# Splitting every load of q, k and v from one DMA of four heads (256 KB) into two of two heads (128 KB)

## Chip, cores, metric

One core of a Trainium2 chip. The metric is the device time of one execution in microseconds (us), as the median of several runs; the profile of one execution is read beside it. On one core a run is called slow when it lies more than 1.5% above the fastest run of the same kernel. Ratios use fast runs alone.

## The reference, cut to what matters

Linear attention with decay over 4 batches, 8 heads, 768 positions and 64 columns, in blocks of 64 with a running state per head, then a highway layer with two 512 x 512 weights. Everything is float32 in and out.

```python
for b in range(nb):
    qb, kb, vb = (q[:, :, sl], k[:, :, sl], v[:, :, sl])
    intra = einsum('bhij,bhjd->bhid', einsum('bhic,bhjc->bhij', qb, kb) * Dmask, vb)
    inter = einsum('bhid,bhde->bhie', qb * lam_pow, kv_state)
    out[:, :, sl] = intra + inter
    kv_state = lam_block * kv_state + einsum('bhsd,bhse->bhde', kb * rev_pow, vb)
...
H = np.maximum(x @ w_h, 0.0); T = 1.0 / (1.0 + np.exp(-(x @ w_t + b_t)))
return T * H + (1.0 - T) * x
```

## The kernel before

The work is cut into 12 stages of 256 positions and all 8 heads. Each stage loads 512 KB each of q, k and v, in two DMAs of 256 KB. Another engine casts a tile to bf16 (kb, qb, vs), and TensorE then transposes and multiplies. The first two stages are handled in halves of four heads; later stages have one tile of eight heads each, with five buffers. All loads and stores go through SyncE's DMA queue, in a fixed order written by hand: all loads first, with the eight weight loads among them, and then the 25 stores.

```python
def load(x, src, n, p, hs):
    b, c = divmod(n, NST)
    for h in range(hs.start, hs.stop, 4):
        nc.sync.dma_start(out=get(x, n, p)[:, h - hs.start:h - hs.start + 4, :],
                          in_=src[b, h:h + 4, c * 2 * C:(c + 1) * 2 * C, :].rearrange("h (p j) d -> p h (j d)", j=J))
...
def fill(eng):      # TensorE's warm-up, 12 times, before the first data arrive
    for i in range(2):
        T.matmul(get("fill")[:, i], lhsT=id128, rhs=id128[:, None, :].to_broadcast([128, NP, 128]), start=True, stop=True)
...
LA = 5              # buffers of a load tile
```

The layer that builds the program gives the DMAs of SyncE and ScalarE eight semaphores in turn; an issue waits until the DMA eight places before it has landed. So eight are in flight at most.

## Time and profile before

| | before |
|---|---|
| time | 113.19 us median (113.16 to 113.62) |
| span in the profile | 110.9 us |
| DMAs issued by SyncE until the last load | 80 |
| last load's issue ends | 72.5 us |
| median from issue to landing of a load | 5.4 us |

How to read it: SyncE's track shows how long it takes to hand a DMA to the queue, not how long the data move. The table of slices shows how full the DMA engines are. The two together tell whether the issue or the engines set the pace. The lines are in the prediction. Some words used there: a DMA lands when its data have arrived and its semaphore, a counter that other engines wait on, says so; a descriptor is one contiguous run of bytes in a DMA, 512 bytes in a load of q, k or v; push-back means that an issue is drawn out because the DMA engines have not yet taken the earlier work; the slack of a tile is the time between its being ready and its first use.

### The profile page before, as it was taken

The page shows a single profiled execution, that of the slowest core. Times are in us where ns is not written, and L with a number is a line of the kernel's source. Part 1 is how long each engine was busy: PE and PEld are TensorE (multiplying, and loading weights), DVE is VectorE, ACT ScalarE, POOL GpSimd, SP SyncE. Part 2 cuts the span into 40 slices and gives each one's busy share as a digit, 9 for nine tenths or more (in the row PEclk, how much of TensorE's full clock was granted, in tenths as well). Part 3 has the DMA queues.
Part 4 walks back from the last instruction along what each step waited for, and adds up shares of the span by engine and source line. Part 5 has one row for each costly group of instructions (what it writes and reads, how often), then busy time and mean ns, then how long its engine had stood idle before and what let it go on. Part 6 is the DMA issues. An engine that isn't in the chain of part 4 may idle for free.

```text
span 110.9 us, 4776 instructions
## 1 busy us (share of the span) xinstructions
PE 101.5 (92%) x2073; PEld 86.3 (78%) x2073; DVE 78.4 (71%) x128; ACT 72.9 (66%) x137; POOL 63.5 (57%) x55
## 2 busy tenths in 40 slices
PE   4996489689999999999999999999999999999960
PEld 1353469578889889888888889999899888889950
DVE  0179896684998899797778854788775797764630
ACT  3574443177288967668695788787878844785780
POOL 6004626263469899988979979899940040401420
PEclk9999965559999999999999999999999999999998
DMA  0999999999999999999999999999995250024263
GB/s 10 267 292 290 290 293 287 293 356 320 253 290 297 288 292 292 290 294 289 293 287 287 279 292 295 292 264 370 392 343 204 107 188 0 6 101 183 101 236 142
DMA packets 43964, 27.57 MB, mean 249 GB/s; under 512 B 1828, under 2 KB 41000, under 8 KB 43944
## 3 DMA queue, kind: packets, MB, share of 16 engines
q1 hardware_dynamic: 43792, 27.27, 88.3%
q8 instruction: 16, 0.26, 1.0%
q14 instruction: 4, 0.03, 0.1%
q10 hardware_dynamic: 152, 0.01, 0.1%
HBM read 20.98 MB, written 6.29 MB: 246 GB/s over the span
## 4 chain that ended last, share of the span: by engine, by line
PE 76%; SPq 11%; DMA 6%; DVE 2%; issue 1%; POOLq 1%; ACT 0%; DVEq 0%
PE w L293 39%; SPq L208 11%; PE w L315 10%; PE w L223 10%; DMA kf<-in_k_dram 6%; PE w L239 5%; PE o L264 5%; PE kv L272 4%; PE o L252 4%; DVE qT L175 1%; POOLq L469 1%; DVE kb L175 1%; DVE hmx L297 0%; ACT o_sb L173 0%; DVEq L175 0%
## 5 line engine op out<-in xcount | busy, mean ns | idle before, releaser
L293 PE MATMUL w<-xT,w_b 128*128 128x256 bf16 (+1 forms) x416 | 46.9, 265 | 0.0
L293 PEld LDWEIGHTS <-w_b 128*128 128x128 bf16 x416 | 36.5, 98 | 4.4
L243 DVE TENSOR_TENSOR m<-w,tri 128x512 bf16<-128x512 f32 x48 | 30.8, 684 | 4.2 <-PE w L239 3.8
L309 POOL TENSOR_TENSOR th<-t_sb,hmx 128x512 bf16<-128x512 bf16 (+1 forms) x13 | 15.1, 1165 | 23.5 <-DVE hmx L297 14.4
L217 POOL TENSOR_TENSOR vs<-vf,pow_k 128x1024 bf16<-128x1024 f32 (+1 forms) x11 | 20.1, 1824 | 12.2 <-DMA vf<-in_v_dram 11.1
L297 DVE SCALAR_TENSOR_TENSOR hmx<-w,xT 128x512 bf16<-128x512 f32 (+1 forms) x26 | 16.5, 646 | 7.7 <-PE w L293 7.4
L217 POOL TENSOR_TENSOR qb<-qf,pow_q 128x1024 bf16<-128x1024 f32 (+1 forms) x11 | 19.2, 1746 | 4.2 <-DMA qf<-in_q_dram 4.2
L306 ACT ACTIVATE w<-w,bt_col 128x256 f32<-128x256 f32 (+1 forms) x26 | 11.2, 432 | 7.6 <-PE w L293 5.7
L173 ACT ACTIVATE xT<-o 128x512 bf16<-128x512 f32 x22 | 12.1, 597 | 3.7 <-PE o L264 2.3
L173 ACT ACTIVATE kT<-w 128x1024 bf16<-128x1024 bf16 (+1 forms) x11 | 10.0, 906 | 6.9 <-PE w L223 6.9
L315 PE MATMUL w<-id,th 128*128 128x128 bf16 x96 | 12.9, 219 | 0.6 <-POOL th L309 0.6
L239 PE MATMUL w<-qT,kT 64*64 64x128 bf16 x384 | 12.8, 231 | 0.7 <-ACT kT L173 0.3
L315 PE MATMUL w<-id,xT 128*128 128x128 bf16 x96 | 12.9, 220 | 0.0
L173 ACT ACTIVATE o_sb<-w 128x512 f32<-128x512 f32 (+1 forms) x17 | 9.6, 575 | 4.8 <-PE w L315 4.6
L306 ACT ACTIVATE t_sb<-w,bt_col 128x256 bf16<-128x256 f32 (+1 forms) x26 | 10.5, 458 | 3.0 <-PE w L293 3.0
L309 DVE TENSOR_TENSOR th<-w,hmx 128x512 bf16<-128x512 f32 (+1 forms) x13 | 8.4, 648 | 4.2 <-ACT w L306 4.0
L223 PE MATMUL w<-id,kb 128*128 128x128 bf16 x96 | 8.5, 231 | 2.8 <-DVE kb L175 1.4
L272 PE MATMUL kv<-vs,kb 64*64 64x64 bf16 x320 | 10.4, 203 | 0.1
L315 PEld LDWEIGHTS <-th 128*128 128x128 bf16 x96 | 9.4, 98 | 0.9 <-POOL th L309 0.8
L239 PEld LDWEIGHTS <-kT 64*64 64x64 bf16 x384 | 9.1, 112 | 1.2 <-ACT kT L173 0.5
L272 PEld LDWEIGHTS <-kb 64*64 64x64 bf16 x320 | 8.8, 117 | 1.3 <-issue 1.0
L315 PEld LDWEIGHTS <-xT 128*128 128x128 bf16 x96 | 9.3, 98 | 0.5
(46 smaller groups left out, 118.9 us busy)
## 6 DMA issues: line engine op xcount, KB each, us to landing
vf<-in_v_dram SPq DMA_DIRECT2D x24, 256.0 KB, 5.4
kf<-in_k_dram SPq DMA_DIRECT2D x24, 256.0 KB, 5.5
qf<-in_q_dram SPq DMA_DIRECT2D x24, 256.0 KB, 5.5
out_dram<-o_sb SPq DMA_DIRECT2D x23, 256.0 KB, 3.5
w_f<-in_moe_w_t_dram SPq DMA_DIRECT2D x4, 256.0 KB, 6.1
w_f<-in_moe_w_h_dram SPq DMA_DIRECT2D x4, 256.0 KB, 6.2
out_dram<-o_sb SPq DMA_DIRECT2D x2, 128.0 KB, 1.9
lam_bc<-in_lam_dram ACTq DMA_DIRECT2D x1, 4.0 KB, 3.5
```

The costliest lines, as they stand in the source:

```text
L173: A.activation(dst, src, AF.Copy)
L208: nc.sync.dma_start(out=get(x, n, p)[:, h - hs.start:h - hs.start + 4, :], in_=src[b, h:h + 4, c * 2 * C:(c + 1) * 2 * C, :].rearrange("h ...
L217: ENG[eng].tensor_tensor(dst[:, hs], in0=get(x, n, p).rearrange("p h (j d) -> p h j d", j=J), in1=pw[:, :, :, None].to_broadcast([128, hs. ...
L223: T.transpose(get(x + "tr", n, p)[:, i, j, :], get(x + "b", n)[:, j, h:h + 2, :], id128)
L239: T.matmul(get("s", n, u, e)[half(b), i, j, :], lhsT=turned("k", n)[half(e), hp, b * C + j:(b + 1) * C:J], rhs=turned("q", n)[half(e), hp, ...
L243: V.tensor_tensor(get("m", n, u)[:, e], in0=get("s", n, u, e), in1=tri[:, None].to_broadcast([128, 2, J, C]), op=ALU.mult)
L272: T.matmul(get("kv", n // NST)[half(e), hp, :], lhsT=get("kb", n)[half(b), j, 2 * hp + e, :], rhs=get("vs", n)[half(b), 2 * hp + e, j, :], ...
L293: T.matmul(get(x, g, js[0])[:, i, :], lhsT=w[:, kc, j * 128:(j + 1) * 128], rhs=get("xT", g)[:, kc, :], start=(kc == 0), stop=(kc == KC - 1))
L297: V.scalar_tensor_tensor(get("hmx", g, js[0]), in0=get("h", g, js[0]), scalar=0.0, in1=get("xT", g)[:, js[0]:js[-1] + 1, :], op0=ALU.max, ...
L306: A.activation(get(*gate(g, js))[:, i, :], get("t", g, js[0])[:, i, :], AF.Sigmoid, bias=bt_col[:, j:j + 1])
L309: ENG[TH[js[0] // len(js) % 2]].tensor_tensor(get("th", g)[:, js[0]:js[-1] + 1, :], in0=get(*gate(g, js)), in1=get("hmx", g, js[0]), op=AL ...
L315: T.matmul(get("x", n, b, p)[:, (j - js[0]) * 128:(j - js[0] + 1) * 128], lhsT=get(x, g)[:, j, r * C:(r + 1) * C], rhs=id128, start=(j == ...
```

## The change

Its intent: a load in smaller pieces lands earlier, so that the first casts can start earlier.

```diff
-        for h in range(hs.start, hs.stop, 4):
-            nc.sync.dma_start(out=get(x, n, p)[:, h - hs.start:h - hs.start + 4, :],
-                              in_=src[b, h:h + 4, ...].rearrange("h (p j) d -> p h (j d)", j=J))
+        for h in range(hs.start, hs.stop, 2):
+            nc.sync.dma_start(out=get(x, n, p)[:, h - hs.start:h - hs.start + 2, :],
+                              in_=src[b, h:h + 2, ...].rearrange("h (p j) d -> p h (j d)", j=J))
```

(The slice of positions is cut; it is the same on both sides.)

More of the change, by code (lines that the diff above doesn't have):

```diff
@@ L206, in load @@
         b, c = divmod(n, NST)
-        for h in range(hs.start, hs.stop, 4):
-            nc.sync.dma_start(out=get(x, n, p)[:, h - hs.start:h - hs.start + 4, :],
-                              in_=src[b, h:h + 4, c * 2 * C:(c + 1) * 2 * C, :].rearrange("h (p j) d -> p h (j d)", j=J))
+        for h in range(hs.start, hs.stop, 2):
+            nc.sync.dma_start(out=get(x, n, p)[:, h - hs.start:h - hs.start + 2, :],
+                              in_=src[b, h:h + 2, c * 2 * C:(c + 1) * 2 * C, :].rearrange("h (p j) d -> p h (j d)", j=J))
     def cast_k(n, p, hs, eng):
```

## The prediction

> **What bounds the kernel now.** I read the overview of engines and slices first, then the chain of work that ended last, then the queue that issues the DMAs (its timeline and its own waits), and at the end the places where a cast waits for a load and a matmul waits for the cast.
>
> ```profile
> span 110.9 us, 4776 instructions
> PE 101.5 (92%) x2073; PEld 86.3 (78%) x2073; DVE 78.4 (71%) x128; ACT 72.9 (66%) x137; POOL 63.5 (57%) x55
> PE   4996489689999999999999999999999999999960
> ...
> DMA  0999999999999999999999999999995250024263
> GB/s 10 267 292 290 290 293 287 293 356 320 253 290 297 288 292 292 290 294 289 293 287 287 279 292 295 292 264 370 392 343 204 107 188 0 6 101 183 101 236 142
> ...
> PE 76%; SPq 11%; DMA 6%; DVE 2%; issue 1%; POOLq 1%; ACT 0%; DVEq 0%
> ...
> vf<-in_v_dram SPq DMA_DIRECT2D x24, 256.0 KB, 5.4
> ```
>
> The reader is to see two limits at once. From about 24 us to the end TensorE is busy in every slice, and it is 76% of the chain. But the 16 DMA engines are as full from 2.8 us to about 72 us, at some 290 GB/s: the loads arrive just in time, and the first 20 us of the chain are loads (SPq 11%, DMA 6%). So a small loss of load rate is not hidden by a long lead. What feeds the DMA engines is one queue, SyncE's:
>
> ```profile
> 12.35 1.71 SPq L208 DMA_DIRECT2D kf<-in_k_dram  x2
> 14.11 1.92 SPq L208 DMA_DIRECT2D vf<-in_v_dram  x2
> 16.07 2.48 SPq L169 DMA_DIRECT2D w_f<-in_moe_w_t_dram  x2
> 18.60 2.01 SPq L169 DMA_DIRECT2D w_f<-in_moe_w_h_dram  x4
> 20.70 2.48 SPq L169 DMA_DIRECT2D w_f<-in_moe_w_t_dram  x2
> 23.22 1.02 SPq L208 DMA_DIRECT2D qf<-in_q_dram  x2
> ```
>
> Columns: start, length, what. SyncE is issuing without a break from 0.8 us to 72.6 us, when the first store goes out. Two kinds of length stand side by side. A 256 KB load mostly takes about 0.83 us to issue (1.71 for two); but two take 1.02, so 0.51 each, when the queue was not full. A load of 256 KB at 300 GB/s is 0.87 us of data. So 0.83 plus the gap of 0.04 is the DMA engines pushing back, and 0.51 is the price of an issue by itself. The issue has had about 0.32 us to spare per load, and the waits that this queue has on semaphores of loads are next to nothing (0.3 us and 0.2 us, once each). Then the far end of the line, at 70 to 76 us:
>
> ```profile
> 69.81 1.90 POOL L217 TENSOR_TENSOR qb<-qf,pow_q 128x1024 bf16<-128x1024 f32 x1 [0.62 <-DMA qf<-in_q_dram]
> 71.66 1.04 POOL L175 CAST kb<-kf 128x1024 bf16<-128x1024 f32 x1
> ...
> 77.47 1.04 POOL L175 CAST kb<-kf 128x1024 bf16<-128x1024 f32 x1
> ```
>
> ```profile
> 75.41 0.62 PE L223 MATMUL w<-id,kb 128*128 128x128 bf16 x8
> 75.86 0.61 PE L223 MATMUL w<-id,qb 128*128 128x128 bf16 x8
> ```
>
> GpSimd's cast that ends at 72.70 is first used by TensorE at 75.41: 2.7 us of slack. For the qb that ends at 71.71 it is 4.15 us, and for the kb that ends at 78.51 it is 6.0 us (used at 84.53).
>
> **What the Trainium skill says.** "Perfetto Trace Analysis", section "What 'DMA-bound' means", separates being bound on the DMA engines from being bound on the DMA sequencer, which shows as an issuing engine's track that is solid DMA slices. This trace has such a solid track, but with slices of 0.83 us where 0.51 us are possible: it is the first kind now. The same page, "DMA Instruction — HWDGE (DVE, Sync)", says the profiled length of an issue is descriptor generation and not the data movement; it agrees, 0.83 us of issue against 5.4 us to landing. "DMA: Bandwidth & Descriptors", section "Rules for kernel authors", advises coalescing small transfers; the change goes the other way, and whether 128 KB is small here is what the sum below decides.
>
> **The change, part by part.** Removed: 72 loads of 256 KB. Added: 144 of 128 KB. The bytes are the same, and so are the 512-byte runs, so the number of data descriptors is the same: 512 per old load, 256 per new one. Order on every compute engine is the same; only names of buffers differ. Each consumer of a tile waits for twice as many semaphores. Such waits are short instructions of 17 ns to 43 ns which the sequencers clear while the previous operation still runs, so I count nothing for them. The program rotates eight DMA semaphores, each issue waiting for the DMA eight places before. Eight in flight were 2 MB, and will be 1 MB.
>
> Cost of one new issue. Three shapes show unblocked, back-to-back issues. A store (128 descriptors) takes 0.45 us, the four w_h loads (256 descriptors) 0.47 us, a load (512) 0.505 us, each with a gap of about 0.045 us. That is 0.495, 0.513 and 0.55 us from start to start: nearly all fixed, about 0.48 us, plus 0.14 ns per descriptor. A new load has the descriptor count of a w_h load, so I take 0.514 us. Two of them cost 1.03 us for what now takes 0.87 us. The DMA engines would need only 0.44 us per 128 KB (some 0.46 with the additional semaphore write). So the issue becomes the bound: 255 GB/s instead of about 300, and the stream of loads and weights (152 issues) lasts 152 x 0.514 = 78.1 us instead of 71.8.
>
> Landing. With the queue no longer full, a load need not stand in line: instead of 5.4 us from issue to landing I estimate 2.6 us, which lies between a lone 256 KB store (2.0 us) and the very first load (4.4 us). Eight issues last 4.1 us, above 2.6, so the eight semaphores should not bind, save at the start: the seventh issue there waits for the small lam load, landing at 4.3 us, where 0.80 + 6 x 0.514 = 3.88. That is 0.46 us lost.
>
> Now the slack, with issue m at 0.80 + 0.46 + (m - 1) x 0.514 + 0.06 for each earlier double wait of the queue (gaps of 0.10 instead of 0.04 now):
> - The kf that ended the load chain at 19.8 us now is issue 32: 17.19 + 2.6 = 19.8 us. No change; before it, the first four tiles land up to 0.8 us earlier, and some from the ninth on up to 0.5 us later.
> - The eight weight loads land up to 2 us earlier, but TensorE is busy then. Nothing.
> - The qf of 69.81: issue 136, 71.2 + 2.6 = 73.8, so 4.0 us late against 4.15 of slack. Nothing yet.
> - The kf of 71.66: issue 140, 73.3 + 2.6 = 75.9, cast until 76.95. TensorE wanted it at 75.41: a stall of about 1.6 us.
> - The last kf: issue 152, 79.6 + 2.6 = 82.2, cast until 83.2; used at 84.53 + 1.6. Hidden. GpSimd's later product (now 81.70 to 82.86, used at 85.03) would end at 86.3, against 85.03 + 1.6. Hidden, narrowly.
> - Stores start at about 80 us instead of 72.6. Twelve output buffers hold them, and the thirteenth copy (about 83.5 us now) needs the first store landed at about 82.5. Hidden.
> After that TensorE alone sets the end, so the stall reaches it whole. The sum: 113.2 + 1.6 = 114.8 us.
>
> **The rivals.** First, hidden anyway: the issue of 256 descriptors takes nearer to 0.42 us (one w_t load did, after a gap). Then the DMA engines stay the bound at about 0.46 us, landings fall from 5.4 to under 4 us, which offsets the late issue, and the time stays at 113 us. For it speaks the slack of several us in most tiles; against it the four equal w_h issues. Second, the issue price does not fall with size at all: 0.55 us each, so the 140th issue is 5.0 us later than I said; the stall is 6 us, near 119.5 us. Against it: the straight line through three shapes. Third, the eight semaphores bind: if a landing takes over 4.1 us with 1 MB in flight, the rate falls to 1 MB per landing time; 4.4 us would give 0.55 us per load and the same 119 us. For it speaks the first load's 4.4 us, against it lone stores at 2.0 us. Fourth, a gain: smaller loads let the first casts start up to 0.8 us earlier. The chain's last load does not profit, so at most a few tenths.
>
> **Range and chances.** An error of 0.01 us in the issue moves the stall by 1.4 us, and 0.5 us in the landing moves it by 0.5 us. Down it is cut off at zero, up it is not. I predict 114.8 us, with 113.2 to 117.5 us for 8 in 10. Slower by over 2% begins at 115.45 us, which needs the issue at 0.519 us: 0.38. Within 2% 0.60, faster 0.02.
>
> **What would show it.** Right: SyncE's load issues near 0.47 us with gaps of 0.045; the first store near 80 us; the GB/s of the middle slices near 255 with DMA below 9 in places; landings of 2 to 3.5 us; a TensorE idle of 1 to 2 us before a transpose of kb near 75 us, and none elsewhere. Wrong: issues that still show push-back (0.4 us with 290 GB/s), or gaps before the issues that are put down to loads (the semaphores), or a stall at the start, before 21 us, instead of near 75.

## The result

The changed kernel takes 127.31 us in the median (126.02 to 128.57, four runs, one of them slow), against 113.19 us. The ratio of the fast runs is 1.120, with a 95% interval of 1.110 to 1.130. A ratio here is the mean time of one kernel's fast runs over the mean of the other's in the same rounds, so it is not quite the ratio of the medians. I had predicted 114.8 us, with 113.2 to 117.5 us for 8 in 10.

The page of the changed kernel: its span, TensorE's share, the slices of TensorE, DMA and GB/s, the chain by engine, and one line of the DMA issues.

```profile
span 126.0 us, 4886 instructions
PE 105.4 (84%) x2073; PEld 88.3 (70%) x2073; DVE 78.8 (63%) x128; ACT 73.0 (58%) x137; POOL 63.6 (50%) x55
PE   5983778839999997998499986990999999999960
...
DMA  2989968899888687857887788786899972024253
GB/s 50 259 237 261 265 187 240 230 350 314 237 252 223 193 224 206 240 160 207 243 233 219 224 213 252 219 245 199 241 337 365 380 280 92 0 88 166 88 213 123
...
SPq 35%; PE 29%; DMA 19%; issue 4%; POOL 4%; DVE 4%; ACT 1%; POOLq 1%; DVEq 0%
...
vf<-in_v_dram SPq DMA_DIRECT2D x48, 128.0 KB, 3.3
```

The DMA engines are no longer full, and TensorE has holes up to three quarters of the span. SyncE's queue has gone from 11% of the chain to 35%, and TensorE from 76% to 29%. A load now lands 3.3 us after its issue instead of 5.4, and the whole is slower all the same. The stretch of the loads in both kernels, with the columns of busy time by engine, then granted clock, DMA share and GB/s; first the kernel before, then the changed one:

```profile
2.80:72.50 69.70, 65.53 (x1349) 54.64 (x1348) 53.87 (x87) 46.12 (x85) 47.83 (x34) 0.93 1.13 292
```

```profile
2.80:91.00 88.20, 73.38 (x1481) 60.70 (x1483) 58.90 (x94) 50.45 (x91) 50.84 (x36) 0.91 0.83 235
```

The same bytes take 88.2 us instead of 69.7, at 235 GB/s instead of 292. (A DMA share above 1 means that packets overlapped on the 16 engines.) Now SyncE's track in the changed kernel, with start, length and what:

```profile
13.09 3.37 SPq L208 DMA_DIRECT2D qf<-in_q_dram  x4
16.50 2.02 SPq L208 DMA_DIRECT2D kf<-in_k_dram  x4
18.57 2.00 SPq L208 DMA_DIRECT2D vf<-in_v_dram  x4
20.62 0.98 SPq L169 DMA_DIRECT2D w_f<-in_moe_w_t_dram  x2
21.64 2.83 SPq L169 DMA_DIRECT2D w_f<-in_moe_w_h_dram  x4
...
25.92 2.53 SPq L208 DMA_DIRECT2D qf<-in_q_dram  x4
28.84 3.05 SPq L208 DMA_DIRECT2D kf<-in_k_dram  x4
```

Four issues take 2.00 us when nothing disturbs them: 0.47 us each, with gaps of 0.045. That is the predicted price. But the first line takes 3.37 us, because one of its four lasts 1.82 us. The fifth line holds one of 1.29 us. In the last two lines SyncE waits between issues for the weight loads, which are still 256 KB each. These are its only sizeable waits on loads, 2.7 us in all:

```profile
SPq L208 <- DMA w_f<-in_moe_w_h_dram: 1.4, 4, 0.4
SPq L208 <- DMA w_f<-in_moe_w_t_dram: 1.3, 4, 0.4
```

I added up all 152 issues of the trace, from the first start at 0.80 us to the last end at 90.97 us. Issues up to 0.55 us count whole, and the 13 longer ones count as 0.47 us each. With the ordinary gaps this gives 76.6 us. The 13 long issues add 10.0 us above that. Ten gaps over 0.15 us add 3.6 us. The sum is 90.2 us. The long issues do not fall just anywhere. The view of the DMA queues, asked for a short stretch around the first of them (14.63 us, in the window from 14.5 to 15.7), shows a transfer on the instruction queue. Its columns are packets, MB and share.

```profile
q8 instruction: 1, 0.02, 7.5%
```

There are 16 such transfers of 16 KB in the whole trace, 11 of them within the load stream. At 10 of these 11 a long issue starts within 0.25 us, and at the other one 0.8 us later. The two long issues that are left (0.78 us at 39.12 us, 0.59 us at 54.62 us) stand beside transfers of 8 KB on a second instruction queue, q14. The kernel before has the transfers of 16 KB too, ten within its load stream, each with an issue of 1.06 to 1.97 us that starts within 0.6 us of it. There the issue of a load at 41.92 us lasts 1.51 us beside a transfer at 41.90 us. The next load is then issued in 0.51 us:

```profile
41.05 2.38 SPq L208 DMA_DIRECT2D kf<-in_k_dram  x2
43.48 0.51 SPq L208 DMA_DIRECT2D vf<-in_v_dram  x1
```

There a load landed over 5 us after its issue, so the DMA engines had work queued and did not notice, and SyncE caught up at 0.51 us an issue. The changed kernel's SyncE is never ahead, so it cannot catch up, and the engines run dry. The view of stretches shows it at the end of a long issue (DMA share and GB/s are its last two columns), first in the kernel before (the issue at 41.92 us), then in the changed one (the issue at 52.76 us, 1.82 us long). Over the eleven transfers of the changed kernel the mean rate falls from some 245 to 90 GB/s about 1.9 us after the transfer's start, counted from the packed trace; in the kernel before it stays at 250 or more.

```profile
43.30:44.10 0.80, 0.80 (x11) 0.72 (x9) 0.80 (x3) 0.60 (x1) 0.80 (x2) 1.00 1.19 302
```

```profile
54.20:55.00 0.80, 0.80 (x35) 0.71 (x24) 0.80 (x3) 0.77 (x3) 0.80 (x1) 1.00 0.28 70
```

### The profile page after: what moved, and what is told of

The parts are those of the page before. It is cut to its first block, busy times and chain, and to the rows that moved or that the text cites. A ratio compares the mean times of both kernels' runs of the same rounds, so it can differ in the third digit from the quotient of the medians.

```text
span 126.0 us, 4886 instructions
## 1 busy us (share of the span) xinstructions
PE 105.4 (84%) x2073; PEld 88.3 (70%) x2073; DVE 78.8 (63%) x128; ACT 73.0 (58%) x137; POOL 63.6 (50%) x55
## 4 chain that ended last, share of the span: by engine, by line
SPq 35%; PE 29%; DMA 19%; issue 4%; POOL 4%; DVE 4%; ACT 1%; POOLq 1%; DVEq 0%
SPq L208 35%; PE w L293 16%; DMA vf<-in_v_dram 7%; DMA kf<-in_k_dram 5%; DMA w_f<-in_moe_w_t_dram 5%; PE w L315 4%; DMA qf<-in_q_dram 2%; PE w L223 2%; PE o L264 2%; PE w L239 2%; DVE hmx L297 2%; PE kv L272 2%; POOL qb L217 2%; POOL vs L217 1%; PE o L252 1%
## 5 line engine op out<-in xcount | busy, mean ns | idle before, releaser
L293 PE MATMUL w<-xT,w_b 128*128 128x256 bf16 (+1 forms) x416 | 48.9, 271 | 0.4 <-DVE m L243 0.4
L293 PEld LDWEIGHTS <-w_b 128*128 128x128 bf16 x416 | 37.5, 100 | 5.8 <-issue 0.8
L223 PEld LDWEIGHTS <-kb 128*128 128x128 bf16 x96 | 6.2, 103 | 9.7 <-POOL kb L175 8.2
```

The lines of the kernel that those rows point to most:

```text
L223: T.transpose(get(x + "tr", n, p)[:, i, j, :], get(x + "b", n)[:, j, h:h + 2, :], id128)
L293: T.matmul(get(x, g, js[0])[:, i, :], lhsT=w[:, kc, j * 128:(j + 1) * 128], rhs=get("xT", g)[:, kc, :], start=(kc == 0), stop=(kc == KC - 1))
```

## The experiments

Theory A: the load stream is bound by SyncE's issuing (0.51 us each, plus a stall at each instruction transfer), and the time follows the end of that stream. Rival B: what matters is that eight DMAs in flight are now 1 MB instead of 2 MB. Rival C: the DMA engines themselves move 128 KB pieces less well. "Last load" below is the end of SyncE's last load issue in the profiled run.

### e1: many issues, large pieces

```diff
             nc.sync.dma_start(out=get(x, n, p)[:, h - hs.start:h - hs.start + 4, :], in_=src[b, h:h + 4, ...])
+            nc.sync.dma_start(out=extra[:, 4 * next(slot):][:, 0:4], in_=src[b, h, ...][:, 0:4])   # 2 KB, never read
```

> Loads stay at 256 KB, but each is followed in the same queue by a load of 2 KB (128 runs of 16 bytes) that nothing reads, so that SyncE issues as many DMAs (152) as the changed kernel. Theory A, the price of issuing: a pair costs 0.55 + 0.495 = 1.045 us to issue against 1.03 us for two half loads, so 72 pairs and 8 weight loads last 79.3 us, plus about 12 us of stalls and waits as in the changed kernel; the last load is issued near 91 us and the time is 125 to 129 us. Theory C, the DMA engines move smaller transfers less well: the data here go in 256 KB pieces, so at most 114 us. Theory B, only eight DMAs (1 MB) in flight: also some 127 us, but SyncE would show gaps put down to waits on loads, well over the 3 us of the changed kernel.

It took 132.16 us, ratio 1.169 (1.162 to 1.176), last load at 94.4 us. All data that are used go in pieces of 256 KB, and it is slower than the changed kernel. Its 9216 small packets do not fill the DMA engines: its slices of DMA are no fuller than the changed kernel's (5 to 9 in most of the load stream). C falls. The packed traces say the same directly: a packet of 512 bytes took 27 ns in the median in the changed kernel and 32 ns in the kernel before, so the engines do not move it more slowly. SyncE's track shows why the size hardly matters:

```profile
62.57 0.38 SPq L211 DMA_DIRECT2D vf<-in_v_dram  x1
62.99 0.50 SPq L213 DMA_DIRECT2D extra<-in_v_dram  x1
63.54 0.43 SPq L211 DMA_DIRECT2D vf<-in_v_dram  x1
64.02 0.50 SPq L213 DMA_DIRECT2D extra<-in_v_dram  x1
```

The issue of 2 KB takes 0.50 us, more than that of 256 KB beside it (0.38 to 0.43 us here, where the prediction read 0.505 us in the kernel before). So the straight line in the number of descriptors, which the prediction drew, is not a law, although it gave the right 0.47 us for the half load. The time is above the 125 to 129 us expected, and the last load is 3 us later than expected: its 16 long issues cost 13.2 us instead of 10 (four of them, 2.0 us in all, have no instruction transfer beside them). SyncE's waits on loads during the load stream add up to 2.8 us, no more than the 3.1 us of the changed kernel (2.7 for weights, 0.4 for v), so B, which called for well over 3 us of them, gets no support. In the changed kernel itself these 3.1 us are all that B could claim of a loss of 14 us.

### e2: some issues moved to ScalarE

```diff
-            nc.sync.dma_start(
+            (nc.scalar if x == "vf" and h % 4 else nc.sync).dma_start(
```

> Half loads as in the changed kernel, but the second half of each v load is issued by ScalarE (24 of 152). Same sizes, same eight semaphores, same 1 MB in flight. Theory A: SyncE issues 128, so its stream is 24 x 0.514 = 12.3 us shorter at best, last load issued near 80 us instead of 90.5, and the time falls to 115 to 120 us (ScalarE pays 0.4 to 0.5 us per issue and may be held up by its waits). Theories B and C: no change, 126 us or more.

It took 141.62 us, ratio 1.240: a miss for A, and no help for B or C either. ScalarE runs its program in order and shares the eight semaphores. In its track (ACTq are its DMA issues) it sits in front of its next copy while it issues v loads and waits for k loads:

```profile
75.39 1.97 ACTq L210 DMA_DIRECT2D vf<-in_v_dram  x2
77.40 1.08 ACT L173 ACTIVATE xT<-o 128x512 bf16<-128x512 f32 x2 [5.41 <-DMA kf<-in_k_dram]
```

SyncE's last load did come at 82.5 us, near the 80 us that A expected, but its stream holds 12.3 us of gaps over 0.15 us, and TensorE's waits that are put down to ScalarE add up to 22.8 us. (The profiled run counts as slow, as do two of the four.) The run changes two things at once, so it decides nothing.

### e3 and e4: fewer half loads

```diff
-        for h in range(hs.start, hs.stop, 2):
+        step = 2 if x in ("qf", "kf") else 4      # e3;  e4:  2 if x == "vf" else 4
+        for h in range(hs.start, hs.stop, step):
```

> Half loads of q and k only, v stays at 256 KB: 128 issues. Theory A: 24 x 0.55 + 104 x 0.514 = 66.7 us of issuing plus about 12 us of stalls and waits, last load issued near 79 us; by the slack worked out in the prediction (about 78 us costs nothing, each us later costs one) 113.5 to 116 us. Theory C, in proportion to the bytes in half loads: 113.2 + 2/3 x 14 = 122.5 us.

> Half loads of v only: 104 issues. Theory A: 48 x 0.55 + 56 x 0.514 = 55.2 us plus 12 us of stalls, 67 us, under the 72 us that the DMA engines take anyway: they stay the bound, the time stays at 113 to 114 us. Theory C, in proportion: 113.2 + 1/3 x 14 = 118 us.

e3 took 118.87 us in the median; three of its four runs count as slow, the fast one took 116.65 us. Its last load came at 82.5 us in a slow run, where A gave 79 us. The fast run lies just above what A gave, and all four lie below C's 122.5 us. e4 took 112.76 us, ratio 0.993 (0.988 to 0.998), last load at 74.2 us in a run that counts as slow; its repetition is e10. A third of the bytes in half loads costs nothing, where C wanted 118 us.

### e5 and e12: do the long issues follow TensorE's instructions?

```diff
-            T.matmul(get("fill")[:, i], lhsT=id128, rhs=id128[:, None, :].to_broadcast([128, NP, 128]), start=True, stop=True)
+            for hp in range(NP):
+                T.matmul(get("fill")[:, i, hp, :], lhsT=id128, rhs=id128, start=True, stop=True, skip_group_check=True)
```

> The changed kernel, with TensorE's 24 warm-up matmuls of 512 columns written as 96 of 128 columns: 144 more TensorE instructions before the first real one, the loads untouched. In every run so far each 16 KB transfer on the instruction queue lies within about 1 us of an issue of SyncE that takes 1.2 to 1.8 us instead of 0.47, the first at 14.6 us. If the transfer is TensorE's instructions and holds up the issue, the first transfer comes earlier, before 12.5 us, and the first long issue comes with it; the later ones move too, always in pairs. If the long issues come from the number of DMAs issued or from data volume, the first stays at the 29th load, at 14 to 15 us. The time stays at 125 to 129 us either way.

> The changed kernel with the rewritten warm-up, with timed rounds: one or two more stalls inside the load stream, none of them hidden: 1 to 3 us above the 127.3 us of the changed kernel, the last load issued near 93 us.

The loads are untouched; only TensorE has 144 more instructions (72 more weight loads and 72 more matmuls) in its warm-up. The first transfer on the instruction queue moved from 14.6 to 8.5 us, and the first long issue moved with it. SyncE's track and the view of the queues in the stretch from 8.4 to 9.6 us:

```profile
7.96 3.11 SPq L209 DMA_DIRECT2D kf<-in_k_dram  x4
```

```profile
q8 instruction: 1, 0.02, 6.0%
```

One of these four issues lasts 1.57 us. In the changed kernel the four issues at this place take 2.00 us. In the changed kernel no such transfer falls in that stretch. All 12 transfers of 16 KB within e5's load stream have a long issue within 0.25 us. So the long issues come with the transfers, the transfers follow TensorE's program, and the number of DMAs issued does not set their place. The reverse holds less strictly: two of e5's 16 long issues, of 0.8 us each at 25.3 and 26.2 us, have no transfer beside them. e5 took 129.54 us in its single run (state unknown), just above the 125 to 129 us expected, last load at 93.9 us. e12, the same kernel in timed rounds, took 129.40 us, ratio 1.134 (1.123 to 1.146), last load at 91.9 us. That is 2 us above the changed kernel's median, but the two were timed in different rounds and the intervals of their ratios overlap, so that an additional stall costs time is not shown here.

### e6 and e7: one part of the program alone

```diff
+        step = 4 if n < 2 else 2      # e6;  e7:  2 if n < 2 else 4
```

> Half loads only from the third stage on; the first two stages keep their twelve loads of 256 KB: 140 issues. Theory A: the stream is bound by the DMA engines for the first 12 us (12 x 0.87 instead of 24 x 0.514: 1.9 us less) and by the issue after that; last load issued near 89 us, 123 to 126 us.

> The complement: half loads in the first two stages only, 92 issues. Theory A: the first 24 issues last 12.3 us instead of 10.5, after that the DMA engines are the bound and 2 MB are in flight again; the stream ends at most 2 us later, which the slack takes; the first casts start up to 0.8 us earlier. 113 us, between 112.3 and 114.5.

e6 took 125.68 us, ratio 1.112 (1.100 to 1.125), last load at 88.5 us. e7 took 114.27 us, ratio 1.014 (1.007 to 1.021), last load at 74.7 us. A caution for e6, e7 and e8, which were timed in the same rounds: one run of the kernel before took 111.63 us there, at a granted clock of 1.0, so that six of its eleven runs count as slow, and the ratios come out high. The median of the eleven is 113.38 us, and e7's is 0.8% above it. Still, nearly all of the loss comes from the ten later stages, for e6 lies 12 us above, far outside that spread. The earlier landing in the first two stages, which was the intent of the change, buys nothing that these runs show.

### e8: larger loads

```diff
+        step = hs.stop - hs.start      # one DMA for the whole tile: 512 KB from the third stage on
```

> The other way: loads of 512 KB from the third stage on, 50 issues. Theory A: the issue was not the bound at 256 KB, so a cheaper issue buys nothing: 112.7 to 113.8 us. If larger transfers move faster in the DMA engines, the middle slices would show over 300 GB/s and the time would fall by a microsecond or more.

It took 114.46 us, ratio 1.015 (1.006 to 1.023), last load at 71.8 us, with some 270 to 305 GB/s in most of the middle slices. Saving 30 issues buys nothing, as A says, because at 256 KB the issue was not the bound. The median is 1.0% above that of the kernel before in the same rounds, slightly worse than I expected, and I did not look into why.

### e9: some issues moved to GpSimd

```diff
-            nc.sync.dma_start(
+            (nc.gpsimd if x == "vf" and h % 4 and n >= 2 else nc.sync).dma_start(
```

> Half loads as in the changed kernel, but the second half of each v load from the third stage on (20 of 152) is issued by GpSimd, whose queue has semaphores of its own, so that SyncE's stream is not tied to another engine's place in its program as it was with ScalarE. SyncE issues 132. Theory A: 20 x 0.6 us (price and share of stalls) less, last load issued by SyncE near 79 to 81 us, the time between 115 and 121 us, the upper end if GpSimd's own issuing (unknown here, perhaps 1 us each) delays its casts. Theories B and C: no gain, 126 us or more.

It took 122.86 us, ratio 1.091 (1.078 to 1.104), last load of SyncE at 82.1 us. The pieces are as small as in the changed kernel, but 20 fewer issues on SyncE bring its stream to an end 9 us earlier and win back 4.5 us of the time. The median is 2 us above A's upper end. GpSimd pays for its issues, two at a time, between its casts:

```profile
40.24 1.46 POOL L208 DMA_DIRECT2D vf<-in_v_dram  x2
```

That is about 10 x 1.46 = 14.6 us on an engine that the casts wait for. GpSimd's queue has semaphores of its own, so this run also lets a little more be in flight; it speaks for A against C, and less cleanly for A against B.

### e10: e4 again

> The half loads of v only, again, to see whether the 0.7% by which they beat the kernel before is real. Theory A has no reason for more than a few tenths of a microsecond at the start; expected 112.3 to 113.5 us, the interval of the ratio touching 1.

113.17 us against 113.18 us, ratio 1.000 (0.992 to 1.009). The gain of e4 was not real. No version that I ran beats the kernel before.

### e11: an additional stall where the queue is deep

The warm-up of e5, on the kernel before.

> The kernel before, loads of 256 KB, with the same rewritten warm-up: 144 more TensorE instructions, one more transfer on the instruction queue. Theory A with stalls that the 2 MB in flight hide: the long issues move with the transfers, first one near 9 us, the last load is issued within 0.7 us of the 72.5 us of before, and the time stays within 1% of the kernel before.

The first transfer came at 10.4 us, with an issue of 1.87 us beside it, and 11 transfers instead of 10 lay within the load stream. The ratio is 0.998 (0.986 to 1.010). The last load was issued at 73.8 us, 1.3 us later than before, where I had allowed 0.7 us. So the stall shows in the stream but not in the time: the slack takes it.

### Taken together

| kernel | DMAs on SyncE to the last load | last load, us | span of the profiled run, us |
|---|---|---|---|
| e8 | 50 | 71.8 | 112.7 |
| before | 80 | 72.5 | 110.9 |
| e11 | 80 | 73.8 | 110.6 |
| e10 | 104 | 74.1 | 111.1 |
| e7 | 92 | 74.7 | 111.7 |
| e3 | 128 | 82.5 | 116.5 |
| e6 | 140 | 88.5 | 122.8 |
| changed | 152 | 91.0 | 126.0 |
| e12 | 152 | 91.9 | 127.5 |
| e5 | 152 | 93.9 | 127.8 |
| e1 | 152 | 94.4 | 130.2 |

Up to about 75 us the end of the load stream costs next to nothing. From e6 to e1 the span grows by 7.4 us for 5.9 us of load stream, so each microsecond costs a little over one. (e2 and e9, where other engines also issue loads, are left out, and e4, which is the kernel of e10; e3's profiled run counts as slow, and the state of e5's is unknown.)

## Why the prediction was wrong

- **The price of an issue.** Right: 0.47 us and a gap of 0.045 for a half load, against 0.51 us in sum as predicted. How it was reached was partly luck: e1 shows 0.50 us for 2 KB.
- **The length of the load stream, "152 x 0.514 = 78.1 us".** This is the step that failed. With its allowances, 0.46 us at the start and 0.72 us for double waits, it put the end of the last issue at about 80 us; it came at 91.0 us. The ordinary issues took 76.6 us, so that part was right. Missing were 10.0 us of long issues beside the instruction transfers. They stood in the profile of before, as ten issues of 1.1 to 2.0 us, and one is in the prediction's own lines (2.48 us for two w_t loads, 1.97 and 0.47). The prediction speaks of two kinds of length, 0.83 and 0.51 us, and passes over this third one. Also missing were the waits for the weight loads, 2.7 us, where I had said that the eight semaphores would bind only at the start. With the ordinary issues alone the stream would have ended at 77.4 us, before the 78.5 us from which a stall begins by the prediction's sum (see below): an estimate from these figures, which no run shows.
- **At the start.** The seventh issue was not held up: it went out at 3.86 us, because the small lam load had landed at 3.5 us instead of 4.3.
- **Landing.** I estimated 2.6 us; the median is 3.3 us. Counted from the packed trace, loads issued in the 2.5 us before a transfer of 16 KB land in 3.7 us (median), those issued in the 2.5 us after its start in 2.7 us, the long ones beside it in 3.5 us, the rest in 3.1 us. So data already under way are late too, and not SyncE's track alone. The weight loads, still 256 KB each, were given the same 2.6 us; they took 5.3 to 5.9 us and landed 2.9 to 3.8 us later than before, where I had said up to 2 us earlier.
- **The slack.** The total is right within 2 us. By the prediction's sum a stall begins when the last issue ends later than about 78.5 us. Set the measured 91.0 us into it and it gives 113.2 + 12.5 = 125.7 us, against a mean of 126.9 us for the fast runs. The stall that I named, before the transposes of the kb whose loads are issues 137 to 140, is there, and it is the longest before a transpose: 2.96 us instead of 1.6, at 88.26 us instead of 75.41. The last kb is hidden, as said (its transposes start at 98.90 us without a wait). But "none elsewhere" was wrong: TensorE waits at many places, 7.4 us in all for GpSimd's kb before transposes and 3.1 us for its vs. That so coarse a sum comes within 2 us is partly luck. The stall that I named:

```profile
88.26 0.62 PE L223 MATMUL w<-id,kb 128*128 128x128 bf16 x8 [2.96 <-POOL kb L175]
```

- **The rivals.** "Hidden anyway" is excluded by the DMA slices, which are no longer full. "The price does not fall with size" holds in e1, but at 0.5 us and not at 0.55 (and its own sum, 1.6 + 5.0 us of stall, gives 119.8 and not 119.5 us). The early gain came (the first kf tile had landed at 5.35 us instead of 6.10) and was worth nothing, as said. Rival B, the depth, is left with the 3.1 us of waits on loads, 2.7 of them at the weights. Whether more semaphores would have bridged the stalls I could not try, because their number is fixed in the building layer.
- **Left open.** That the long issues come with the transfers of instructions is shown by e5, e11 and e12, where the two moved together. By what mechanism one holds up the other, whether in SyncE or by way of the DMA engines, and why a long issue costs anything from 0.3 to 1.35 us more than usual, no run here tells.

## What to carry to other kernels

Before cutting DMAs smaller, compare the price of one issue (here 0.51 us, almost whatever the size) with the time that its bytes take in the DMA engines (here 0.87 us for 256 KB, so by estimate 0.44 us for 128 KB): once the first is the larger, the issuing queue sets the pace however short each landing becomes. Count the irregular long issues in as well; here a deep queue hid them, and the change that emptied the queue made them visible. The slack of each consumer tells from which end of the stream on a loss is paid in full.

## What the Trainium skill lacked or had wrong

- "DMA: Bandwidth & Descriptors", section "Issuing engines are not separate DMA queues", calls the time to initiate a DMA usually small relative to the DMA itself. Here it was 0.51 us against an estimated 0.44 us of data for 128 KB, and it became the bound.
- The same page, "Rules for kernel authors", says that under 64 KB one pays mostly overhead. Here loads of 128 KB cost 12% when SyncE issued all of them, and nothing when only v was cut so (e10, ratio 1.000): above that border the number of issues decided, and not the size alone.
- No page that I found says that a DMA issue stalls beside an instruction transfer: 0.47 us became 0.8 to 1.8 us, at 11 of 11 transfers. "Runtime: NRT & Kernel Launch", section "Instruction fetch mechanics", has the refill of instruction memory in blocks of 16 KiB, which agrees with the packets of 16 KB here, and calls the cost of crossing into the next block mostly hidden. For SyncE it was not: 0.3 to 1.35 us each.
- "Perfetto Trace Analysis", section "DMA Optimizations", says that splitting DMAs may let some start sooner, and that the whole may end sooner if the DMA engines are generally idle. Here they were full (share 1.13), so its condition was not met: the first tile did land 0.8 us sooner, and e7, which splits the early loads alone, gained nothing. Its advice to spread DMAs over more engines when descriptor generation is the limit fits e9 (122.9 instead of 127.3 us) and not e2 (141.6 us). The two differ in what else the second engine has to do and in whether it shares SyncE's semaphores; which of these decides is not shown.
